# Reordering one core's instruction lists in an mLSTM and squared-ReLU kernel: scores ahead of attends, the tenth chunk's loads ahead of the eighth's x, joins ahead of squares, and another order of the PSUM banks

## The chip, the cores and the metric

The kernel runs on one core of a Trainium2 chip. A core has a matrix engine (TensorE, PE in the tables, with its weight loads listed apart as PEld), three engines that work on elements (VectorE or DVE, ScalarE or ACT, GpSimd or POOL), and SyncE (SP), which here issues all DMA transfers of the main part from one queue, in program order. Every engine carries out its own list of instructions strictly in order, and waits by semaphores for the others.

The metric is device microseconds of one launch. A chunk below is 128 rows of one batch's sequence with all 8 heads, a group is 256 tokens (two chunks) of the feed-forward part.

## The reference

Two stages run one after the other, all in float32.

```python
# mLSTM cell: B=4, H=8, S=768, D=40; for each t of the sequence, with a running stabiliser m
C = f_stab * C + i_stab * outer(v_t, k_t)
n = f_stab * n + i_stab * k_t
y_t = sigmoid(o_gate_t) * (C @ q_t) / max(|n . q_t|, 1)
# bridge: y (B, H, S, D) -> x (3072 tokens, 320)
# FFN: w_in (320, 2048), w_out (2048, 320)
out = relu(x @ w_in) ** 2 @ w_out
```

## The kernel before

**Chunks.** The recurrence over 768 steps is carried out in 6 chunks of 128 rows per batch, 24 in all, in order. For a chunk s the kernel loads k, q, v, the output gate and a row of decay sums A that is spread over all partitions (`load_A`, L334, tile A_bc, two buffers). POOL masks A (L359), and ACT makes W = exp(A + b) from it in 8 instructions (`weigh`, L383) and eA = exp(A) (`decays`, L369). PE multiplies k and q (`scores`, L423, into tile tp), DVE multiplies this by W (`weighted`, L436, two tiles P_sb), and PE multiplies P_sb by v and eA*q by the state C of the chunk before (`attend`; in the later form `attend_turned`, L522 with C, L511 for the new state, L533 with P_sb, into tile numT). The state moves on by C*decay plus the new products (L550, with POOL's `decay_C`, L489).

**The turned path.** From chunk 6 or 7 on, transposes are made with DMA and DVE. `pair_up` (4 DMAs, L287) copies k and q to a DRAM scratch, `load_squares` (4 DMAs, L309) brings them back in squares into kqT, one of two buffers, and `turn_kq` (DVE, L316) turns these. The attend's numerator goes numT, turned by DVE into tn (L544), `store_num` (L556) to DRAM, `load_num` (4 DMAs, L561) back, `normalise_turned` (DVE, L573 to L582) divides and applies the gate to give x_sb, `store_rows` (L608) and `load_rows` (4 DMAs, L613) bring x back as squares of xT, and `turn_squares` (DVE, L620) ends the turn. Then xT is ready for the feed-forward part.

**The feed-forward part.** FFN1 of a group has four steps (L644 with 32 and L655 with 16 matmuls in a batch, h_ps); ACT takes the relu into r_sb (L670), DVE the square into g (L677). FFN2 of group 0 is plain (L684). FFN2 of the other groups (`ffn2_fast`) makes the 2 by 2 block product with 7 products of 16 matmuls (L738), in four steps. These need sums of g (`sums`, L733) and of the weights (`sums_of_weights`, L712 to L719). The products go to two PSUM banks X and Y that are held through two steps; ACT copies (L758, L763) and DVE adds (L754) collect them in y_sb, which has three buffers for the two that a group uses. Steps 2 and 3 each store half of the group's result (L774, L779).

**Weights.** w_in and w_out are rounded while they come in, in 26 pieces. For a piece ACT makes two words (`words`, L195 and L197), DVE three steps and POOL the last add (`join`, L206, L210, L211, L215), and the fetch of a later piece follows on SP (L186).

**The order.** No scheduler moves anything: within each engine the order is that of the Python text. After a prologue, a loop `for u in range(8)` (L873) handles chunks 2 to 5, two turns for each, with FFN1 of groups 0 and 1 and the rounding of weights between. In it the three PSUM pools ps_at (3 banks), ps_h (3) and ps_o (2) are open. They are closed then, and ps_at and ps_h with 4 banks each follow. The second loop (L982) runs over a list of parts: n counts them, `which` is 1 for an FFN1 step and 2 for an FFN2 step. From n = 8 on, eight parts make a group's round: r = 0 and 1 are steps 0 and 1 of `ffn2_fast`, r = 2 to 5 the four FFN1 steps of the group two further, r = 6 and 7 the steps 2 and 3. FFN1 runs in pairs of steps: the matmuls L644 of both, L655 of both, and between them and the relus a "tiled" section, in which the attend of a chunk and the score of the next are placed. b = 7 + 2*(n//8) is the chunk of the round's first tiled section, b + 1 that of its second. The call `attended(s)` issues store_num, the next load of v and k, load_num and pair_up on SP. SP's and DVE's instructions in a round are thus in the order of the calls at r = 0 to 7.

Of the kernel before, what the change touches and what calls it, by code (L numbers as in the profile page):

```python
# [15 lines left out]
PSUM = bass.MemoryType.PSUM  # L16
# [13 lines left out]
def kernel(  # L30
# [49 lines left out]
    work = ctx.enter_context(tc.tile_pool(name="work", bufs=2))  # L80
    xts = ctx.enter_context(tc.tile_pool(name="xts", bufs=2))
    banks = ExitStack()
    ps_at = banks.enter_context(tc.tile_pool(name="ps_at", bufs=3, space=PSUM))
    ps_h = banks.enter_context(tc.tile_pool(name="ps_h", bufs=3, space=PSUM))
    ps_o = banks.enter_context(tc.tile_pool(name="ps_o", bufs=2, space=PSUM))
    ctx.enter_context(tc.manual_schedule())
    first = ExitStack()
    gates = first.enter_context(tc.tile_pool(name="gates", bufs=1))
# [225 lines left out]
    def turn_kq(s):  # L314
        t = kqT_b[s % NKT][:].rearrange("p n j t -> p (n j t)")
        nc.vector.transpose(t, t)  # L316
# [264 lines left out]
        nc.vector.tensor_tensor(x3, x3, dm[:].unsqueeze(2).to_broadcast([P, H, D]), op=ALU.mult)  # L581
        nc.vector.tensor_copy(x[:, DM:], x[:, DM - KR : DM])  # L582

    def normalise(s):
        d = st[s]
        num = d["num"]
        if num is not d["hp"]:
            nc.vector.tensor_tensor(num[:], num[:], d["hp"][:], op=ALU.add)
        dm = work.tile([P, H], F32, name="dm")
        nc.vector.tensor_scalar(dm[:], num[:, :, D], scalar1=-1.0, scalar2=1.0, op0=ALU.mult, op1=ALU.max)  # L590
        nc.vector.tensor_tensor(dm[:], dm[:], num[:, :, D], op=ALU.max)
        nc.vector.reciprocal(dm[:], dm[:])

        x = d["x"] = work.tile([P, 3 * P], F32, name="x_sb")
        x3 = x[:, :DM].rearrange("p (h d) -> p h d", d=D)
        nc.vector.tensor_tensor(x3, num[:, :, :D], d["og"], op=ALU.mult)
        nc.vector.tensor_tensor(x3, x3, dm[:].unsqueeze(2).to_broadcast([P, H, D]), op=ALU.mult)
        nc.vector.tensor_copy(x[:, DM:], x[:, DM - KR : DM])
# [183 lines left out]
    def do(f, s):  # L782
        if 0 <= s < NT:
            f(s)
# [66 lines left out]
    sigmoid(1)  # L851
    attend(0)
    rounding.step()
    normalise(0)
    mask(2)
    attend(1)
    normalise(1)
    load(3)
    load_A(3)
# [13 lines left out]
    for u in range(8):  # L873
        s = 2 + u // 2
        relu_half()
        if u % 2 == 0:
            if u == 0:
                ffn1(0, 0)
                scores(s)
                weighted(s)  # L880
                relu_half()
                rounding.step()
            else:
                turn_rows(s - 1)
                scores(s)
                ffn1(u // 4, u % 4)
            if u == 2:
                rounding.words()
            if u > 0:
                weighted(s)  # L890
            if u == 2:
                mask(s + 1)
                rounding.join()
                rounding.join()
                weigh(s + 1, masked=True)
                rounding.words()
            else:
                weigh(s + 1)
                if u > 0:
                    square_half()  # L900
        else:
            load_A(s + 2)
            for r in {1: (4,), 3: (5, 6), 5: (7,), 7: ()}[u]:
                load(r)
            if u == 5:
                for r in range(4, 8):
                    sigmoid(r)
            attend(s)
            if u in (1, 3):
                if u == 3:  # L910
                    square_half()
                normalise(s)
                rounding.join()
            else:
                rounding.join()
                normalise(s)
            for r in {5: (8,), 7: (9,)}.get(u, ()):
                load(r)
            for r in {5: (7,), 7: (8,)}.get(u, ()):
                pair_up(r)  # L920
            if u > 4:
                load_o(2 * s)
                load_o(2 * s + 1)
            transposes(s + 1)
            rounding.words()
            if u == 7:
                ffn1_main(1, 3)
                turn_rows(5)
                ffn1_rest(1, 3, st["half"][0])
            else:  # L930
                ffn1(u // 4, u % 4)
            square_half()
        if u < 4:
            load_o(4 + u)
        while rounding.done < NEXT[u]:
            rounding.step()
    relu_half()
    square_half()
    load_A(8)
    load_squares(7)  # L940
# [18 lines left out]
    assert LAST[-1] == len(pieces)  # L959


    def attended(s):
        do(store_num, s)
        do(load, s + 4)
        do(load_num, s)
        do(pair_up, s + 3)

    def ffn1_batch(g, i, tiled=lambda: None):
# [13 lines left out]
    for n, (which, g, i) in enumerate(parts):  # L982
# [11 lines left out]
        if n in (2, 5):  # L994
            attend_turned(s)
            decays(s + 1)
            mask(s + 1)
            if n > 4:
                turn_kq(s + 1)
            decay_C(s + 1)  # L1000
            if s > X_SQ:
                turn_squares(s - 1)
            attended(s)
        if n == 6:
            scale_q(s + 1)
        if 5 <= n < 8:
# [1 line left out]
        if n == 6:  # L1008
            sums(1, ALL, (1, 2))
        if n == 8:  # L1010
            decays(9)
            mask(9)
            turn_kq(9)
            load_squares(10)
            load_A(10)
            sums_of_weights(3)
            sums(1, ALL, (3,))
        if n == 9:
            attend_turned(8)
            score(9)  # L1020
            decay_C(9)
            attended(8)
            turn_squares(7)
# [3 lines left out]
        if r == 0 and g > 1:  # L1027
            do(turn_squares, b - 2)
            sums(g, ALL, (3,))
        elif r == 1 and g > 1:  # L1030
            do(turn_squares, b - 1)
        elif r == 4:
            do(scale_q, b + 1)
            do(turn_kq, b + 2)
        elif r == 5:
            do(normalise_turned, b)
            do(store_rows, b)
        elif r == 7 and g < NG - 1:
            sums(g + 1, ALL, (2,))
            do(normalise_turned, b + 1)  # L1040
            do(store_rows, b + 1)
# [5 lines left out]
        if which == 1:  # L1047
            ffn1_main(g, i)
            if i % 2 == 0:
                st["held"] = st["half"]  # L1050
            elif r is None:
                ffn1_batch(g, i)
                if n != 3:
                    square_half()
                    square_half()
            else:
                x = b + i // 2

                def tiled():
                    do(attend_turned, x)  # L1060
                    do(score, x + 1)

                ffn1_batch(g, i, tiled)
                do(decay_C, x + 1)
        elif g == 0:
            ffn2(g, *divmod(i, 2))
        else:
            ffn2_fast(g, i)

        if n in (2, 6):  # L1070
            masked_W(s + 1)
            if n < 4:
                turn_kq(s + 1)
                scale_q(s + 1)
            normalise_turned(s)
            store_rows(s)
            load_squares(s + 2)
            load_rows(s)
            load_A(s + 2)
        if n == 7:  # L1080
            for t in range(8, 12):
                sigmoid(t)
        if n == 8:
            masked_W(9)
        elif n == 9:
            load_A(11)
            load_o(12)
            load_o(13)
            decays(10)
            mask(10)  # L1090
        elif n == 10:
            normalise_turned(8)
            store_rows(8)
        if r == 0 and g > 1:
            do(decays, b + 1)
            do(mask, b + 1)
            square_half()
        elif r == 1:
            if g > 1:
                do(pair_up, b + 2)  # L1100
            square_half()
            if g < NG:
                sums(g, ALL, (4,))
            do(scale_q, b)
            do(turn_kq, b + 1)
        elif r == 2:
            do(masked_W, b + 1)
            do(load_squares, b + 2)
            if n == 10:
                load_rows(8)  # L1110
        elif r == 3:
            do(decays, b + 2)
            do(mask, b + 2)
            attended(b)
            if b % 4 == 3:
                for t in range(b + 1, min(b + 5, NT)):
                    sigmoid(t)
        elif r == 4:
            square_half()
            square_half()  # L1120
            do(masked_W, b + 2)
            do(load_A, b + 3)
        elif r == 5:
            do(store_num, b + 1)
            do(load_rows, b)
            do(load_num, b + 1)
            do(load, b + 5)
            for t in range(b + 5, min(b + 7, NT)):
                load_o(t)
        elif r == 6:  # L1130
            do(load_squares, b + 3)
        elif r == 7:
            do(load_A, b + 4)
            do(load_rows, b + 1)
# [35 lines left out]
```

## Time and profile before

| | us |
|---|---|
| median of 8 runs | 537.05 |
| lowest, highest run | 533.98, 537.86 |
| the profiled run, whole time | 537.25 |
| span of its records | 535.5 |
| PE busy (share of the span) | 515.9 (96%) |
| PEld busy | 449.0 (84%) |
| DVE busy | 329.2 (61%) |
| ACT busy | 192.4 (36%) |
| POOL busy | 88.1 (16%) |
| mean granted clock of PE | 0.984 |

The profile is of one execution. The span is the time from its first to its last record; the run's time holds 1.75 us more. A row of a timeline gives the start, the length, the engine, the line of the kernel, the operation with the tile that it writes and the tiles that it reads, the number of instructions joined in the row (x16), and in brackets the idle time of the engine ahead of them and what ended it. PEclk is the clock that PE was granted, 1.00 being full speed. The chain of waits is followed backwards from the end: each piece is what the next one waited for.

### The profile page before, as it was taken

To read this page: it belongs to the slowest core of one execution; us is meant where nothing else is said; L and a number is where in the kernel's file an instruction comes from. 1 tells how busy PE (TensorE), PEld (TensorE's weight loads), DVE (VectorE), ACT (ScalarE), POOL (GpSimd) and SP (SyncE) were. 2 spreads that over 40 slices of the span, in tenths; PEclk is the share of its full clock that TensorE was granted. 3 is DMA by queue.
4 is the path that set the end of the run, shared out by engine and by line. 5 is a ranking of instruction groups with operands and counts; after the bars stand their busy time and mean duration, and the time that the engine had idled before them with its cause. 6 is when DMAs were issued, how large, how long until landed. Compare 5 with 4: busy or idle time off the path is not lost.

```text
span 535.5 us, 10368 instructions
## 1 busy us (share of the span) xinstructions
PE 515.9 (96%) x3932; PEld 449.0 (84%) x3933; DVE 329.2 (61%) x638; ACT 192.4 (36%) x460; POOL 88.1 (16%) x110
## 2 busy tenths in 40 slices
PE   9997999999949999999999999999999999999997
PEld 4875888786748898897897898897898898998997
DVE  8579988769744773664764773764764764341451
ACT  3776486361534403713413703413613301102100
POOL 3346653221202110110110110100200100000000
PEclk9998899999969999999999999999999999999999
DMA  9999698967487775776775785775673230200000
GB/s 197 219 197 203 153 192 187 206 149 148 100 165 164 160 143 118 157 133 128 156 136 121 156 141 120 167 130 126 155 155 63 76 87 21 63 12 1 26 26 24
DMA packets 239394, 68.06 MB, mean 127 GB/s; under 512 B 185744, under 2 KB 233872, under 8 KB 239344
## 3 DMA queue, kind: packets, MB, share of 16 engines
q1 hardware_dynamic: 239248, 67.20, 60.0%
q8 instruction: 31, 0.51, 0.4%
q10 hardware_dynamic: 96, 0.20, 0.1%
q14 instruction: 19, 0.16, 0.1%
HBM read 55.08 MB, written 17.86 MB: 136 GB/s over the span
## 4 chain that ended last, share of the span: by engine, by line
PE 67%; DMA 15%; DVE 7%; SPq 6%; issue 3%; ACT 1%; POOL 0%; DVEq 0%; POOLq 0%; ACTq 0%
PE h_ps L644 23%; PE h_ps L738 22%; PE h_ps L655 7%; DMA x_rows<-x_sb 4%; PE tp L423 3%; SPq L613 3%; DMA xT<-x_rows 3%; DMA out_dram<-y_sb 2%; DMA kq<-num_rows 2%; PE numT L533 2%; PE hp L459 2%; DMA A_bc<-a_rows 2%; PE idle L797 2%; PE numT L522 1%; DMA num_rows<-tn 1%
## 5 line engine op out<-in xcount | busy, mean ns | idle before, releaser
L644 PE MATMUL h_ps<-xT,w_in 128*128 128x256 f32 x768 | 175.8, 385 | 7.3 <-POOL w_in L215 3.4
L644 PEld LDWEIGHTS h_ps<-xT,w_in 128*128 128x128 f32 x768 | 144.9, 192 | 30.8 <-DVE y_sb L754 5.2
L670 ACT ACTIVATE r_sb<-h_ps 128x512 f32<-128x512 f32 x96 | 49.8, 598 | 126.7 <-PE h_ps L655 74.2
L738 PE MATMUL h_ps<-w_out,g 128*128 128x160 f32 x528 | 77.7, 305 | 3.4 <-ACT y_sb L758 3.4
L738 PEld LDWEIGHTS h_ps<-w_out,g 128*128 128x128 f32 x528 | 75.0, 195 | 3.8 <-ACT y_sb L758 3.7
L677 DVE TENSOR_TENSOR g<-r_sb 128x512 f32<-128x512 f32 x96 | 64.4, 721 | 11.7 <-ACT r_sb L670 11.6
L383 ACT ACTIVATE W_sb<-A_bc,b_T 128x128 f32<-128x128 f32 x176 | 53.8, 388 | 21.2 <-POOL A_bc L359 21.0
L738 PE MATMUL h_ps<-T,S 128*128 128x160 f32 x352 | 52.3, 302 | 0.0
L738 PEld LDWEIGHTS h_ps<-T,S 128*128 128x128 f32 x352 | 48.8, 190 | 1.5 <-ACT r_sb L670 0.7
L655 PE MATMUL h_ps<-xT,w_in 64*128 64x256 f32 x384 | 49.0, 391 | 0.0
L655 PEld LDWEIGHTS h_ps<-xT,w_in 64*128 64x128 f32 x384 | 34.8, 186 | 12.1 <-issue 9.1
L754 DVE TENSOR_TENSOR y_sb<-y_sb,h_ps 128x160 f32<-128x160 f32 x44 | 13.8, 315 | 45.9 <-PE h_ps L738 45.9
L359 POOL TENSOR_SCALAR_AFFINE_SELECT A_bc<-A_bc 128x1024 f32<-128x1024 f32 x22 | 25.5, 1160 | 83.4 <-ACT kq L369 72.9
L758 ACT COPY y_sb<-h_ps 128x160 f32<-128x160 f32 x11 | 3.2, 293 | 99.8 <-PE h_ps L738 99.8
L544 DVE STREAM_TRANSPOSE tn<-numT 128x256 f32<-128x256 f32 x36 | 15.6, 446 | 37.8 <-PE numT L533 37.2
L436 DVE TENSOR_TENSOR P_sb<-tp,W_sb 128x512 f32<-128x512 f32 x46 | 29.7, 686 | 10.2 <-PE tp L423 6.8
L620 DVE STREAM_TRANSPOSE xT<-xT 128x384 f32<-128x384 f32 x18 | 10.3, 572 | 41.3 <-DMA xT<-x_rows 41.3
L423 PE MATMUL tp<-kqT 40*128 40x128 f32 x384 | 28.7, 290 | 4.6 <-issue 3.4
L423 PEld LDWEIGHTS tp<-kqT 40*128 40x128 f32 x384 | 24.4, 193 | 8.9 <-issue 6.4
L395 POOL TENSOR_TENSOR vw<-va,W_sb 128x328 f32<-128x328 f32 x20 | 16.8, 839 | 84.1 <-ACT W_sb L383 73.1
L738 PE MATMUL h_ps<-w_out,S 128*128 128x160 f32 x176 | 25.7, 299 | 0.0
L738 PE MATMUL h_ps<-T,g 128*128 128x160 f32 x176 | 25.7, 299 | 0.0
(119 smaller groups left out, 592.3 us busy)
## 6 DMA issues: line engine op xcount, KB each, us to landing
A_bc<-a_rows SPq DMA_DIRECT2D x23, 512.0 KB, 5.2
raw<-in_moe_w_out_dram SPq DMA_DIRECT2D x16, 320.0 KB, 3.5
num_rows<-tn SPq DMA_DIRECT2D x18, 256.0 KB, 2.3
kq<-num_rows SPq DMA_DIRECT2D x72, 64.0 KB, 2.1
kqT<-kq_rows SPq DMA_DIRECT2D x34, 128.0 KB, 3.2
raw<-in_moe_w_in_dram SPq DMA_DIRECT2D x8, 512.0 KB, 4.9
kq<-in_k_dram SPq DMA_DIRECT2D x24, 160.0 KB, 3.8
va<-in_v_dram SPq DMA_DIRECT2D x24, 160.0 KB, 4.1
```

The lines of the kernel that those rows point to most:

```text
L359: nc.gpsimd.affine_select(A[:], A[:], compare_op=ALU.is_ge, fill=-1e30, base=0, pattern=[[0, H], [1, P]], channel_multiplier=-1,)
L383: nc.scalar.activation(d["W"][:, i * n + h, :], A[i][:, h, :], AF.Exp, bias=b_T[:, b, c, i * n + h : i * n + h + 1],)
L395: nc.gpsimd.tensor_tensor(d["vw"][:], d["va"][:], d["W"][:, :, P - 1 : P].to_broadcast([P, H, D1]), op=ALU.mult,)
L423: nc.tensor.matmul(sc[i][:, j, :], lhsT=d["kT"][rows, j, :], rhs=d["qT"][rows, j, :], start=True, stop=True,)
L436: nc.vector.tensor_tensor(t, d["sc"][i], d["W"][:, heads, :], op=ALU.mult)
L544: nc.vector.transpose(to[:, 2 * i : 2 * i + 2], numT[i][:, :2, :].rearrange("p c t -> p (c t)"))
L613: nc.sync.dma_start(t[r * SQ : (r + 1) * SQ].rearrange("p (b a) -> p b a", a=SQ), x_d[s, :, :, r * SQ : (r + 1) * SQ].rearrange("c (n p) a ...
L644: nc.tensor.matmul(hs[i][:, n, :], lhsT=w_in[:, a, fb * P : (fb + 1) * P], rhs=xT[:, :, a, :], start=(n == 0 and a == 0), stop=False,)
L655: nc.tensor.matmul(hs[i][:, n, :], lhsT=w_in2[rows, 2 * pp + n, :], rhs=xT[rows, :, 2, :], start=False, stop=(n == 1),)
L670: nc.scalar.activation(rs[-1][:], h[:], AF.Relu)
L677: nc.vector.tensor_tensor(g4[:, :, i, :], r[:], r[:], op=ALU.mult)
L738: nc.tensor.matmul(to, lhsT=lhsT[:, p], rhs=rhs[:, p, :], start=(start and p == 0), stop=(p == NPAIR - 1), skip_group_check=True,)
```

## The change

The change adds and removes no instruction. It moves them within the engines' lists, and opens the PSUM pools in another order.

- PSUM pools of the first loop: ps_o is opened first, then ps_at, ps_h. The banks are then o 0-1, at 2-4, h 5-7 instead of at 0-2, h 3-5, o 6-7. The second loop's pools lie at banks 0-3 and 4-7 in both, so another bank follows each of the old ones.
- First loop: `sum_of_h` is split off `normalise`, and stands ahead of the join where the join now stands ahead of the rest of normalise (u = 1 as well as 5 and 7). At u = 1 the squares follow the joins of the weights. At u = 7 the last square and relu come ahead of the words.
- The tenth chunk (s = 9): its `load_squares` and `load_A` are issued by `attended(7, early=True)`, after load_num(7) and ahead of pair_up(10), of a store of y, and of store_rows(7) and load_rows(7). Its `decays`, `mask` and `turn_kq` are called at the end of part 7 instead of in part 8.
- `score` stands ahead of `attend_turned` in part 9 and in each tiled section, so the scores' matmuls and DVE's two P_sb are ahead of the attend's matmuls, its two tn and the update of C.
- `turn_squares(b - 1)` moves from part r = 1 to r = 2, after masked_W and load_squares.

```diff
+    ps_o = banks.enter_context(tc.tile_pool(name="ps_o", bufs=2, space=PSUM))
     ps_at = banks.enter_context(tc.tile_pool(name="ps_at", bufs=3, space=PSUM))
     ps_h = banks.enter_context(tc.tile_pool(name="ps_h", bufs=3, space=PSUM))
-    ps_o = banks.enter_context(tc.tile_pool(name="ps_o", bufs=2, space=PSUM))
...
-            if u in (1, 3):
-                if u == 3:
-                    square_half()
+            if u == 3:
+                square_half()
+            sum_of_h(s)
+            if u == 3:
                 normalise(s)
-                rounding.join()
-            else:
-                rounding.join()
+            rounding.join()
+            if u != 3:
                 normalise(s)
...
                 ffn1_rest(1, 3, st["half"][0])
+                square_half()
+                relu_half()
             else:
                 ffn1(u // 4, u % 4)
-            square_half()
+                if u > 1:
+                    square_half()
...
         while rounding.done < NEXT[u]:
             rounding.step()
-    relu_half()
+        if u == 1:
+            square_half()
     square_half()
...
-    def attended(s):
+    def attended(s, early=False):
         do(store_num, s)
         do(load, s + 4)
         do(load_num, s)
+        if early:
+            load_squares(s + 2)
+            load_A(s + 2)
         do(pair_up, s + 3)
...
-            attended(s)
+            attended(s, early=(n == 5))
...
         if n == 8:
-            decays(9)
-            mask(9)
-            turn_kq(9)
             load_squares(10)
...
         if n == 9:
+            score(9)
             attend_turned(8)
-            score(9)
...
-        elif r == 1 and g > 1:
-            do(turn_squares, b - 1)
...
                 def tiled():
+                    do(score, x + 1)
                     do(attend_turned, x)
-                    do(score, x + 1)
...
             store_rows(s)
-            load_squares(s + 2)
+            if n == 2:
+                load_squares(s + 2)
             load_rows(s)
-            load_A(s + 2)
+            if n == 2:
+                load_A(s + 2)
         if n == 7:
             for t in range(8, 12):
                 sigmoid(t)
+            decays(9)
+            mask(9)
+            turn_kq(9)
...
             do(load_squares, b + 2)
+            if g > 3:
+                do(turn_squares, b - 1)
```

More of the change, by code (lines that the diff above doesn't have):

```diff
@@ L582, in normalise_turned, with sum_of_h @@
         nc.vector.tensor_copy(x[:, DM:], x[:, DM - KR : DM])
-    def normalise(s):
+    def sum_of_h(s):
         d = st[s]
@@ L588, in normalise @@
             nc.vector.tensor_tensor(num[:], num[:], d["hp"][:], op=ALU.add)
+    def normalise(s):
+        d = st[s]
+        num = d["num"]
         dm = work.tile([P, H], F32, name="dm")
@@ L853 @@
     rounding.step()
+    sum_of_h(0)
     normalise(0)
@@ L856 @@
     attend(1)
+    sum_of_h(1)
     normalise(1)
```

## Prediction

> **What bounds the kernel now.** I read the page first. TensorE (PE) is busy almost throughout, so other engines count only where PE waits for them.
>
> ```profile
> PE 515.9 (96%) x3932; PEld 449.0 (84%) x3933; DVE 329.2 (61%) x638; ACT 192.4 (36%) x460; POOL 88.1 (16%) x110
> PE   9997999999949999999999999999999999999997
> PEclk9998899999969999999999999999999999999999
> ```
>
> A slice is 13.4 us. Slices 4 and 12 (PE 7 and 4) stand out, and the granted clock sinks around both. So next I read PE's timeline for its idle times, and for records slower than their own pace (L644 0.216 us each, L738 16 in 2.17, L423 16 in 1.09).
>
> ```profile
> 50.18 1.22 PE L644 MATMUL h_ps<-xT,w_in 128*128 128x256 f32 x2 [2.20 <-POOL w_in L215]
> 52.65 5.11 PE L644 MATMUL h_ps<-xT,w_in 128*128 128x256 f32 x14 [1.25 <-POOL w_in L215]
> ...
> 99.50 1.16 PE L423 MATMUL tp<-kqT 40*128 40x128 f32 x16 [1.25 <-ACT r_sb L670]
> ...
> 152.16 2.17 PE L423 MATMUL tp<-kqT 40*128 40x128 f32 x16 [3.35 <-issue]
> 157.70 6.79 PE L738 MATMUL h_ps<-w_out,g 128*128 128x160 f32 x32 [3.36 <-ACT y_sb L758]
> 164.33 7.07 PE L644 MATMUL h_ps<-xT,w_in 128*128 128x256 f32 x32
> ...
> 249.04 1.99 PE L644 MATMUL h_ps<-xT,w_in 128*128 128x256 f32 x8 [0.93 <-DVE y_sb L754]
> ```
>
> There are four kinds of loss: weights at 50, a bank at 98, the tenth chunk at 149 to 164, and a short wait in the first FFN1 part of a steady group. 14 L644 in 5.11 instead of 14 x 0.216 = 3.02 is the halved clock. The busy times by stretch (length, PE, PEld, DVE, ACT, POOL, PEclk, DMA share, GB/s) show what precedes it:
>
> ```profile
> 46.10:49.50 3.40, 1.88 (x23) 1.28 (x19) 3.37 (x4) 2.30 (x5) 3.32 (x4) 1.00 1.26 170
> 49.50:56.40 6.90, 4.97 (x11) 3.54 (x12) 6.76 (x9) 3.83 (x8) 4.45 (x4) 0.51 0.59 168
> 97.30:100.70 3.40, 2.15 (x25) 1.58 (x25) 2.07 (x5) 3.40 (x9) 1.24 (x3) 1.00 0.65 123
> ```
>
> A stretch of 3.4 us with PE busy 1.88 (idle 1.52) was followed by half speed, one with 2.15 (idle 1.25) was not. A fall cost 2.1 at 50 (5.11 - 3.02) and 3.4 at 152 (L423 2.17 - 1.09, L738 6.79 - 4.34).
>
> [...]
>
> **A. Joins ahead of squares (25 to 56 us).** FFN1(0,2) waits for w_in pieces 5 and 6: 2.2 and 2.0 idle, 2.1 by the clock. Joins 6 and 7 now precede the two L677 (45.61 to 47.99). But POOL's add of piece 5 stands behind vw, Cd and C (L395, L473, L478, 45.15 to 48.73) whatever DVE does, and ACT's words for piece 6 end at 46.6. [...] Ends: 0.3 (POOL's queue alone rules) and 4 (idle also falls under 1.5 and the clock stays: 1.9 + 2.1). L206 took 1.10 and L210 1.37 beside POOL, against 0.42 and 0.43 for the same forms alone; the joins stay in that company, so I stay near the low end. Squares 2.4 later are covered: their first reader (FFN2) is 50 us on.
>
> [...]
>
> **B. Bank order and relu first.** score(6) at 99.50 waits 1.25 for the relu whose bank it takes; that relu stood behind two `words` on ACT. Now it takes another bank, freed by ACT's copy of xT at 97.7, and follows L655 at 98.18: gain 1.3 (0.5 if the next FFN1 meets the second relu at 99.2). Elsewhere banks rotate with the same depth: 0.
>
> **C. The tenth chunk.** The chain of waits names it:
>
> ```profile
> 143.72 0.38 SPq L608
> ...
> 147.36 0.61 SPq L613
> ...
> 150.42 4.27 DMA A_bc<-a_rows
> ...
> 156.05 0.64 ACT kq L369
> 156.70 0.63 ACT kq L369
> 157.35 0.30 ACT y_sb L758
> 157.70 6.79 PE h_ps L738 x32
> ```
>
> SP is stuck at store_rows(7) (L608) until x is ready at 143.72, and squares(9) (4 L309) and A(9) (L334) stand behind it. So turn_kq(9) waits until 150.82 and score(9) to 152.16; exp(A) begins at 156.05, and on ACT the y_sb copy, which step 1's product needs, stands behind it. PE loses 3.35 + 1.08 + 3.36 + 2.3 = 10.1. After, the five issues (3.10 + 0.47) follow load_num(7) at 136.5: L309 to 139.6, L334 to 140.1, landing (4.3 to 5.4) 144.4 to 145.5. turn_kq(9) (1.25) follows L716 at 145.1 to 146.4, before score(9) at 146.8. ACT ends the sigmoids at 144.6, then table load and L369 (2.6) to 148, the copy to 148.3; attend(8) follows score(9), to 149.9; step 1 runs 149.9 to 154.2. POOL's mask (1.1) and W(9) (2.44) end at 151.5, P_sb(9) at 152.5. xT(7) is the next due: pair_up(10) and L692 (3 us) now fill SP's idle time 139.7 to 143.7, L608 is hardly later, L613 loses the 3.1 of L309 ahead of it but waits for x_rows, and the turn ends near 154. FFN1(3,0) starts at 154.2 to 154.7 instead of 164.33: gain 9.8 (5 if these loads land at 149, where score(9) waits 2 and the clock falls).
>
> Then SP must carry the same transfers in 10 us less. It is almost full from 130 to 190, so y stores and the next loads fall behind in the first group: I give back 2.0 (0 to 4.5; the upper end is SP's own idle time of 4.06 at 139.66 to 143.72, used up).
>
> **D. turn_squares(b-1) from step 1 to after masked_W.** L620 stood ahead of the y_sb add and waited for xT's landing:
>
> ```profile
> 208.60 0.58 DVE L620 STREAM_TRANSPOSE xT<-xT 128x384 f32<-128x384 f32 x1 [7.51 <-DMA xT<-x_rows]
> 209.10 0.28 DVE L754 TENSOR_TENSOR y_sb<-y_sb,h_ps 128x160 f32<-128x160 f32 x1
> ...
> 240.09 0.33 DVE L754 TENSOR_TENSOR y_sb<-h_ps,y_sb 128x160 f32<-128x160 f32 x1 [1.05 <-DMA out_dram<-y_sb]
> ```
>
> The first FFN1 part lacks the bank that this add frees. From x24 at 203.65 to x8 at 209.44 is 5.79, 24 x 0.216 = 5.18: 0.61 lost; in the next groups 1.09, 1.12, 0.40, 0.89. Gain 4.1. Its reader is the next group, so its new place, behind turn_kq(b+1) (213.5), costs nothing.
>
> **E. Score ahead of attend.** PE's work is the same. On DVE the two P_sb(b+1) come ahead of tn(b), and take over the two buffers that attend(b)'s L533 reads. In the group at 213.29 (end of the first L655): score to 214.38, attend to 215.6, then P_sb 1.29, then tn 0.89: end 218.1 instead of 215.48, so 2.65 later. On this path hang, by the chain of waits: num_rows 3.21, L561 on SP, kq 2.43, normalise 2.3, x_rows 3.75, L613 on SP, L561, and behind them on SP the y1 store (L774) at 236.76, landing 3.20. The third row above waits for that landing, as y_sb has three buffers, and step 1's second product needs the add: it ended at 240.42 for a product at 240.60, and in the next groups 0.6, 1.9, 0.9, 1.9, 1.9 ahead. With 1.9 to 2.65 more: 0.9 to 2.3 of PE wait at this group, 0.2 to 1.8, 0 to 1.5, 0.6 to 1.6, then none (no o_gate loads ahead of the store). Ends 1.7 and 7.2, taken 4.4. A wait past 1.5 may also halve the clock (2.1 to 3.4).
>
> **Sum.** -1.0 - 1.3 - 9.8 - 4.1 + 2.0 + 4.4 = -9.8. The profiled execution took 537.25 (span 535.5 and 1.75 around it), 0.2 over the median of 537.05: 537.25 - 9.8 = 527.5 us.
>
> **Rivals.**
> - *E costs nothing* (0.25). SP has idle stretches before L613, and the store may be issued as early as now. Then 537.25 - 16.2 + 2.0 = 523; with A's clock kept (-3) 520. Against it: slack of 0.2 in the group at 240.
> - *SP decides* (0.15). C's loads land at 149 (gain 5), the backlog gives back 4.5, E 4.4, others as forecast: -1.0 - 1.3 - 5 - 4.1 + 4.5 + 4.4 = -2.5: 534.7; with half of C's shortfall 532.
> - *Slower* (0.07). Step 1's wait for the y1 store is worst in all four groups (7.2), and each wait takes a half-clock window with it (4 x 2.8), with the backlog at 4.5: 22.9 against 16.2 gained, 544. It decides from the third fall of the clock on (4.5 + 7.2 + 3 x 2.8 = 20.1, over 16.2 + 1.6). For it: 1.52 idle was enough at 49. Against it: only the first group reaches 1.5 by my middle values.
> - *It does not do what it says* (0.04). The early loads wait for a buffer of kqT or A_bc still read, so C remains, with D paid out by E: about 537. Against it: the last readers of both buffers, W(7) and score(7), end at 119.4 and 121.
>
> **How the numbers follow.** Forecast 527.5 with 0.49. The likeliest cases reach from 520 to 532; with the SP case's 534.7 the range is 519 to 535.5, leaving out the slower and the nothing case and A's and E's best ends together. About 0.3% (1.6 us) is what a measurement of this kernel can tell from no change: faster 0.89 (the first three), same 0.04 (the last), slower 0.07.
>
> **What would show it.** PE's L423 after 146.8 without idle, and no half clock at 152: C. L754 of step 0 directly behind its product and no idle ahead of the x8 of L644: D. A wait of L738 for DVE L754, in turn for out_dram<-y_sb, near 230, 270 and 310: E. The two waits for L215 hardly shorter: A. It is wrong if the loads of chunk 9 land after 147, or if clocks fall in the steady groups.

## The result, and the profile after

| | before | after |
|---|---|---|
| median, us | 535.93 (32 runs) | 529.48 (11 runs) |
| lowest, highest | 533.98, 538.2 | 526.14, 533.69 |
| profiled execution, us | 537.25 | 526.66 |
| span, mean granted clock | 535.5, 0.984 | 524.9, 0.993 |
| PE, DVE, POOL busy | 515.9, 329.2, 88.1 | 510.4, 334.0, 92.2 |

The ratio of the medians is 0.9879 with a 95% interval of 0.9858 to 0.9900: the change takes 6.5 us off. The two profiled executions differ by more, 10.6 us, because the one after is among the quick ones. The executions after spread over 7.5 us, and their granted clock goes with it: 0.996 at 526.1 and 526.3, 0.990 to 0.994 at 528 to 531.5, 0.984 at 533.7. In the clock records of the two profiles the half speed is 0.50; by that, as an estimate, a mean of 0.984 instead of 0.996 is 0.012 x 525 / 0.5 = 12.6 us more at half speed, where up to half is lost. The ratios below leave out one execution of the run y_early (533.8), which lies over 1.5% above the fastest of its kernel.

Lines below L588 have moved by 4 (L644 is L648, L738 is L742, L754 is L758). PE's timeline of the kernel after, the rows that answer to those of before:

```profile
49.20 0.98 PE L648 MATMUL h_ps<-xT,w_in 128*128 128x256 f32 x2 [1.25 <-POOL w_in L215]
51.66 5.56 PE L648 MATMUL h_ps<-xT,w_in 128*128 128x256 f32 x14 [1.48 <-POOL w_in L215]
...
98.95 7.17 PE L648 MATMUL h_ps<-xT,w_in 128*128 128x256 f32 x32 [0.33 <-ACT r_sb L674]
...
145.14 1.16 PE L423 MATMUL tp<-kqT 40*128 40x128 f32 x16
...
148.16 4.61 PE L742 MATMUL h_ps<-w_out,g 128*128 128x160 f32 x32
152.86 7.17 PE L648 MATMUL h_ps<-xT,w_in 128*128 128x256 f32 x32
...
174.42 1.26 PE L423 MATMUL tp<-kqT 40*128 40x128 f32 x16 [0.60 <-PE h_ps L659]
...
193.90 2.44 PE L742 MATMUL h_ps<-w_out,g 128*128 128x160 f32 x16 [3.05 <-DVE y_sb L758]
...
232.54 2.44 PE L742 MATMUL h_ps<-w_out,g 128*128 128x160 f32 x16 [0.36 <-DVE y_sb L758]
...
271.98 2.44 PE L742 MATMUL h_ps<-w_out,g 128*128 128x160 f32 x16 [0.25 <-DVE y_sb L758]
...
311.38 2.44 PE L742 MATMUL h_ps<-w_out,g 128*128 128x160 f32 x16 [0.21 <-DVE y_sb L758]
...
351.56 2.44 PE L742 MATMUL h_ps<-w_out,g 128*128 128x160 f32 x16 [1.90 <-DVE y_sb L758]
```

The two long idle times and the half clock around 152 to 164 (0.50 from 151.9 to 162.2 before, 1.00 from 152 to 157 after) are gone, and so are the waits of the L648 x8. New are the waits of step 1's second product (L742) for DVE's add: the mechanism that part E forecast, and ahead of them one of 3.05 at 193.90, for which E had no term (C's "I give back" had one).

The matmuls of the feed-forward part have the same order in both kernels, so the start of the same matmul in both traces gives a ledger. FFN1(g,p) is the first layer of group g from its step p on, "gained" how much sooner a place is reached, "step" what was gained since the row above:

| place | before | after | gained so far | step |
|---|---|---|---|---|
| end of FFN1(0,2) (A) | 57.68 | 57.16 | 0.5 | 0.5 |
| FFN1(2,0) (B) | 100.60 | 98.95 | 1.6 | 1.1 |
| FFN1(3,0) (C) | 164.33 | 152.86 | 11.5 | 9.8 |
| second product, first group | 201.47 | 193.90 | 7.6 | -3.9 |
| the same, next groups | 240.60 | 232.54 | 8.1 | 0.5 |
| | 281.11 | 271.98 | 9.1 | 1.1 |
| | 321.65 | 311.38 | 10.3 | 1.1 |
| | 360.46 | 351.56 | 8.9 | -1.4 |
| end | 532.33 | 521.75 | 10.6 | 1.7 |

Within a group the same comparison, read every 16 matmuls, separates D from E: 0.72, 1.19, 1.22, 0.40 and 0.99 gained where the L644 x8 had waited (D), 0.52, 0.41, 0.38 and 2.06 lost at the second product (E), and 0.20 gained at each of 13 tiled sections, which nothing in the prediction had.

### The profile page after: what moved, and what is told of

The parts are those of the page before. It is cut to its first block, busy times and chain, and to the rows that moved or that the text cites. A ratio compares the mean times of both kernels' runs of the same rounds, so it can differ in the third digit from the quotient of the medians.

```text
span 524.9 us, 10358 instructions
## 1 busy us (share of the span) xinstructions
PE 510.4 (97%) x3932; PEld 448.0 (85%) x3933; DVE 334.0 (64%) x638; ACT 194.0 (37%) x460; POOL 92.2 (18%) x110
## 4 chain that ended last, share of the span: by engine, by line
PE 69%; DMA 12%; SPq 8%; DVE 6%; issue 2%; ACT 2%; POOL 1%; DVEq 0%; ACTq 0%; POOLq 0%
PE h_ps L648 25%; PE h_ps L742 19%; PE h_ps L659 7%; DMA out_dram<-y_sb 3%; DMA kq<-num_rows 3%; PE tp L423 3%; SPq L561 3%; PE h_ps L688 3%; DMA num_rows<-tn 3%; DMA x_rows<-x_sb 2%; SPq L617 2%; PE hp L459 2%; PE numT L533 2%; PE idle L801 2%; PE numT L522 1%
## 5 line engine op out<-in xcount | busy, mean ns | idle before, releaser
L648 PE MATMUL h_ps<-xT,w_in 128*128 128x256 f32 x768 | 174.8, 385 | 3.8 <-POOL w_in L215 2.7
L648 PEld LDWEIGHTS h_ps<-xT,w_in 128*128 128x128 f32 x768 | 145.4, 192 | 26.4 <-POOL w_in L215 3.6
L742 PE MATMUL h_ps<-w_out,g 128*128 128x160 f32 x528 | 76.9, 300 | 5.8 <-DVE y_sb L758 5.8
L742 PEld LDWEIGHTS h_ps<-w_out,g 128*128 128x128 f32 x528 | 73.0, 190 | 7.3 <-DVE y_sb L758 7.0
L681 DVE TENSOR_TENSOR g<-r_sb 128x512 f32<-128x512 f32 x96 | 68.7, 766 | 10.0 <-ACT r_sb L674 10.0
L742 PE MATMUL h_ps<-T,S 128*128 128x160 f32 x352 | 52.3, 302 | 0.0
L742 PEld LDWEIGHTS h_ps<-T,S 128*128 128x128 f32 x352 | 48.8, 190 | 1.6 <-ACT r_sb L674 0.8
L659 PE MATMUL h_ps<-xT,w_in 64*128 64x256 f32 x384 | 49.0, 391 | 0.0
L659 PEld LDWEIGHTS h_ps<-xT,w_in 64*128 64x128 f32 x384 | 34.8, 186 | 12.1 <-issue 9.1
L758 DVE TENSOR_TENSOR y_sb<-y_sb,h_ps 128x160 f32<-128x160 f32 x44 | 14.1, 320 | 47.0 <-PE h_ps L742 47.0
L359 POOL TENSOR_SCALAR_AFFINE_SELECT A_bc<-A_bc 128x1024 f32<-128x1024 f32 x22 | 29.4, 1334 | 68.9 <-ACT kq L369 67.5
L395 POOL TENSOR_TENSOR vw<-va,W_sb 128x328 f32<-128x328 f32 x20 | 17.7, 887 | 77.2 <-ACT W_sb L383 62.9
L489 POOL TENSOR_TENSOR Cd<-C,kq 128x164 f32<-128x164 f32 x15 | 7.0, 464 | 118.6 <-DVE C L550 104.9
L423 PEld LDWEIGHTS tp<-kqT 40*128 40x128 f32 x384 | 24.8, 188 | 3.3 <-issue 1.1
L423 PE MATMUL tp<-kqT 40*128 40x128 f32 x384 | 26.4, 276 | 0.6 <-PE h_ps L659 0.6
L369 ACT ACTIVATE kq<-A_bc 64x512 f32<-64x512 f32 x30 | 18.8, 628 | 19.7 <-DMA A_bc<-a_rows 17.8
L742 PE MATMUL h_ps<-T,g 128*128 128x160 f32 x176 | 25.7, 299 | 0.0
L742 PE MATMUL h_ps<-w_out,S 128*128 128x160 f32 x176 | 25.7, 299 | 0.0
```

What stands on the lines that cost most here:

```text
L359: nc.gpsimd.affine_select(A[:], A[:], compare_op=ALU.is_ge, fill=-1e30, base=0, pattern=[[0, H], [1, P]], channel_multiplier=-1,)
L369: nc.scalar.activation(e[rows], st[s]["A"][0][rows, PR * i : PR * (i + 1), :], AF.Exp)
L395: nc.gpsimd.tensor_tensor(d["vw"][:], d["va"][:], d["W"][:, :, P - 1 : P].to_broadcast([P, H, D1]), op=ALU.mult,)
L423: nc.tensor.matmul(sc[i][:, j, :], lhsT=d["kT"][rows, j, :], rhs=d["qT"][rows, j, :], start=True, stop=True,)
L648: nc.tensor.matmul(hs[i][:, n, :], lhsT=w_in[:, a, fb * P : (fb + 1) * P], rhs=xT[:, :, a, :], start=(n == 0 and a == 0), stop=False,)
L659: nc.tensor.matmul(hs[i][:, n, :], lhsT=w_in2[rows, 2 * pp + n, :], rhs=xT[rows, :, 2, :], start=False, stop=(n == 1),)
```

## The experiments

Ratios are to the kernel before on the same chip, with 95% intervals. "The first group" is that of FFN1(3,0) and the FFN2 steps behind it. What it "gives back" is the time from the start of FFN1(3,0) to step 1's second product, less the 37.14 (201.47 - 164.33) of before; it is 3.90 (193.90 - 152.86 - 37.14) in the profile above.

**after_again**, the changed kernel once more.

> The changed kernel itself, for another profile of it and as the base for the runs beside it. Both theories: about 529.5 us. In its profile the five waits of PE for DVE's y_sb add (3.05, 0.36, 0.25, 0.21, 1.90 us in the first profile) come again, each within 1.5 us of its first value; if this execution is slower than 526.7, the granted clock is lower in proportion (0.01 of mean clock, 5 us at half speed more, is worth 2 to 2.6 us).

0.9869 (0.9825 to 0.9913); the profiled execution took 531.02. Four waits came again (2.45, 1.06, 0.22, 1.92), the fifth was under 0.2. The first group gave back 6.6, as the score at 175.95 waited 2.40 instead of 0.60 and the clock fell behind it (0.76 from 175 to 182; the 16 of L533 at 178.30 took 1.96 instead of 1.07). PE's timeline of this execution has a row that the first profile has at full speed:

```profile
354.25 3.75 PE L742 MATMUL h_ps<-w_out,g 128*128 128x160 f32 x16 [1.92 <-DVE y_sb L758]
```

16 in 3.75 instead of 2.44: here the clock fell behind the wait of 1.92 (0.93 from 350 to 356, 0.74 from 356 to 361). In the first profile, with 1.90, it stayed at 1.00 (351 to 356). Such falls, there in one execution and absent in another, are a likely source of the spread; the executions without a profile can't show it.

**attend_first**, E undone (here in the tiled sections; part 9 likewise).

```diff
-                    do(score, x + 1)
                     do(attend_turned, x)
+                    do(score, x + 1)
```

> The changed kernel with part E undone: attend ahead of score again in part 9 and in each tiled section. Theory 1 (E makes tn, and through SP's list the y1 store, 2 to 2.6 us late): the five waits shrink from 5.8 in sum to 1.5 or less, while the 0.2 us that each tiled section had gained comes back as a loss (13 x 0.2 = 2.6); 526.5 to 528.5. Rival (SP's list is overfull after the tenth chunk's gain, E has no part in it): the 3.05 stays above 2.5, and the time is 530 to 532.

0.9845 (0.9802 to 0.9888), no different from the changed kernel within the intervals. Against the first profile the ledger shows +0.20 at each tiled section, and -0.52, -0.42, -0.38, -2.06 at the second products: so much of theory 1 holds. But the first group gave back 9.0:

```profile
176.43 0.67 PE L522 MATMUL numT<-kq,C 40*64 40x128 f32 x16 [2.60 <-DVE kq L484]
...
185.61 2.44 PE L742 MATMUL h_ps<-w_out,S 128*128 128x160 f32 x16 [1.54 <-DVE y_sb L758]
...
198.79 3.82 PE L742 MATMUL h_ps<-w_out,g 128*128 128x160 f32 x16 [4.22 <-DVE y_sb L758]
```

So the 3.05 in the first group is not E's: without E it is 4.22. There the rival was right, and the median of 530.71 lies in its 530 to 532.

**y_early**, the y1 store sooner on SP.

```diff
             do(load_num, b + 1)
-            do(load, b + 5)
-            for t in range(b + 5, min(b + 7, NT)):
-                load_o(t)
         elif r == 6:
+            do(load, b + 5)
+            for t in range(b + 5, min(b + 7, NT)):
+                load_o(t)
```

> The changed kernel with the loads of v, k and the output gates of part r = 5 issued after step 2 of the FFN2 and not before it, so that SP issues the y1 store (L778) right behind load_num(b+1), 2.0 to 4 us sooner in the four groups that load gates. Theory 1 (the store's place in SP's list makes PE wait): waits of 3.05 and 1.90 fall below 1, the three of 0.2 to 0.4 vanish; 524 to 526. Rival (the landing itself, or another reader of the bank, holds the add): waits change by less than 0.5, 529 to 530.

0.9784 (0.9735 to 0.9833), which is lower than after_again's, but the two intervals overlap. In the profiled execution the three larger waits remained, 3.64, 0.61 and 2.12. The store was issued right behind load_num as meant (345.33), so its place alone does not make PE wait.

**four_y**, four y_sb tiles from a pool that has room, used in turn.

```diff
-            st["y"] = [ffn.tile([P, DM], F32, name="y_sb", bufs=3) for _ in range(2)]
+            st["y"] = [next_y() for _ in range(2)]
```

> The changed kernel with four y_sb buffers instead of three, so that step 0's add (u12) writes a buffer whose store landed a group before. Theory 1: the five waits for DVE's y_sb add vanish (5.8 us in the profiled execution), and with them what they cost in clock in other executions; 523 to 525. Rival (the add is late for another reason: DVE's place behind normalise and sums): at least half of the waits remain, 527 to 530.

0.9759 (0.9720 to 0.9799): the median is 5.6 us under after_again's on the same chip, and the intervals do not meet, so the fourth buffer is worth something in this kernel. Its profiled execution (529.95) is the slowest of six. In it the waits at 194, 272 and 311 are gone; 0.52 at 235 and 2.13 at 353 are not, and in the first group the score waits 2.78 at 177.11 instead. DVE's timeline tells why the wait at 353 stays:

```profile
348.30 1.11 DVE L573 TENSOR_SCALAR dm<-kq 128x8 f32<-128x8 f32 x1 [4.48 <-DMA kq<-num_rows]
...
352.78 0.32 DVE L767 TENSOR_TENSOR y_sb<-h_ps,y_sb 128x160 f32<-128x160 f32 x1
```

normalise(b+1) (L573 and on) stands ahead of the add (here L767) on DVE, and waits for the landing of num(b+1), the same late chain. The add has two predecessors that E delays, the store and this one; I had seen one. With the store out of the way the other still holds it at 353.

**tn_first**, PE in the new order, DVE in the old (part 9 likewise).

```diff
-                    do(score, x + 1)
+                    do(scores, x + 1)
                     do(attend_turned, x)
+                    do(weighted, x + 1)
```

> The changed kernel with the scores' matmuls still ahead of the attend's on PE, but on DVE tn(b) and the update of C ahead of the two P_sb(b+1). Theory 1 (E's cost is DVE's order, its small gain is PE's order): the 0.2 us of each tiled section stays, and of the waits for DVE's y_sb add those in the groups at 232, 272, 311 and 351 vanish, as with attend first; the first group's stays at 2 to 4.5. About 3 us under the changed kernel of the same chip (ratio to before 0.980 to 0.983). Rival (the gain of 0.2 came with DVE's order, or a tn 1.1 us later than before is still too late): either the sections take 0.2 us longer again, or 0.2 to 1 us of wait remains in at least three of these groups.

0.9776 (0.9737 to 0.9814). The 0.20 of each section stays, the waits at 232, 272 and 311 vanish, and of that at 351 remains 1.62, where a gate load ahead of the y1 store took 2.07 us to issue on SP. So the small gain belongs to PE's order and the three small losses to DVE's; the largest, at 351, stays with DVE in the old order, and whose it is this run leaves open. The first group gave back 7.5.

**c_only**, C alone on the kernel before.

> The kernel before with part C alone. Theory 1: PE's loss from 148.65 to 164.33 goes (9.9 us by step 1's start of FFN1), and 4 to 5.5 come back in the first group, from SP's list: a wait of the score near 174 and of step 1's second product near 195, without E. Ratio to before 0.988 to 0.992. Rival (the first group's waits are E's work): the first group gives back less than 2, and the ratio is 0.981 to 0.985.

0.9957 (0.9930 to 0.9985): C alone is worth 2.3 us. Its ledger shows 10.0 gained at step 1's two products ahead of FFN1(3,0), and 8.0 given back in the first group, with 1.65 more just behind it, where 16 of L738 took 4.03 (the third row):

```profile
179.20 0.67 PE L522 MATMUL numT<-kq,C 40*64 40x128 f32 x16 [1.54 <-DVE kq L484]
...
188.14 2.44 PE L738 MATMUL h_ps<-w_out,S 128*128 128x160 f32 x16 [1.31 <-DVE y_sb L754]
...
201.70 4.03 PE L738 MATMUL h_ps<-w_out,g 128*128 128x160 f32 x16 [4.61 <-DVE y_sb L754]
```

The mechanism was as expected; its size, 8.0 and 1.65, was about twice the 4 to 5.5 that I took.

**sp_light**, two gate loads moved from part 9 to part 12.

> The changed kernel with the gate loads of chunks 12 and 13 (two L324, 2.36 us of SP) issued in part 12 instead of part 9, behind the squares of chunk 11 and the x of chunk 8. Theory 1 (in the first group SP's list is the bound): x store, squares(11) and num(9) are issued 2 to 2.4 us sooner, the score's wait near 174 falls to 0 from 0.6 to 2.8, the y_sb wait near 194 falls below 1.5; 3 to 4 us under the changed kernel. Rival (the landing times of the transfers, shared among 16 engines, are the bound, and not their issue): waits change by less than 1 us.

0.9894 (0.9860 to 0.9928). The score waited 0.70 (0.60 and 2.40 in the two profiles of the changed kernel), and the add's wait rose to 5.03 (from 3.05 and 2.45). On SP the moved loads (179.55 to 181.7) now stood ahead of the store of x of chunk 9, ready at 179.8 and issued at 181.83. The work was moved from one place of the same late chain to another. This run could not decide between the theories.

**fill**, matmuls on zeros ahead of the waits at 48 to 53.

```diff
+        if (g, pp) == (0, 2):
+            fill(4)
...
+                if (g, pp) == (0, 2) and (i, n) == (0, 1):
+                    fill(6)
```

> The changed kernel with 4 and 6 matmuls on zeros (128x512, into a bank of ps_o) ahead of the two waits of FFN1(0,2) for the weights' adds, so that PE is busy in most of the 1.25 and 1.48 us. It computes nothing that is used. Theory 1 (a wait of 1.2 to 1.8 us here halves the clock): the 14 matmuls after the second wait take 3.0 to 3.3 us instead of 4.7 to 5.6, and no half clock shows between 48 and 60; 1.5 to 2.5 us under the changed kernel. Rival (the clock falls here for another reason than idle time): 14 in 4.7 to 5.6 as before, time as the changed kernel's.

0.9867 (0.9794 to 0.9941), nothing gained. My second fill was misplaced: the wait of 1.77 lies between the two matmuls ahead of it, so it remained, and the six fills ran behind it at half speed (2.68 for six). The clock fell for one stretch (51.6 to 55.0 at 0.53) after one with PE busy 1.52 of 3.4. It settles nothing about what a well placed fill is worth.

**e_only**, E alone on the kernel before.

> The kernel before with part E alone. Theory 1: waits of step 1's second product for DVE's y_sb add appear in the groups at 240, 281 and 321 (0.2 to 1 each) and at 360 (1 to 2.3), sum 2.5 to 4.5, against 2.6 gained from PE's order in 13 sections: within 2 us of before, ratio 0.997 to 1.004. Rival (E is the source of the change's gain): ratio under 0.993.

1.0183 (1.0142 to 1.0224): 10 us slower, far outside what either theory gave. DVE's and PE's timelines show where it goes:

```profile
212.50 0.58 DVE L620 STREAM_TRANSPOSE xT<-xT 128x384 f32<-128x384 f32 x1 [7.34 <-DMA xT<-x_rows]
213.01 0.28 DVE L754 TENSOR_TENSOR y_sb<-y_sb,h_ps 128x160 f32<-128x160 f32 x1
...
216.14 1.24 DVE L316 STREAM_TRANSPOSE kqT<-kqT 128x1024 f32<-128x1024 f32 x1
```

```profile
204.02 3.82 PE L738 MATMUL h_ps<-w_out,g 128*128 128x160 f32 x16 [3.08 <-DVE y_sb L754]
...
213.34 1.99 PE L644 MATMUL h_ps<-xT,w_in 128*128 128x256 f32 x8 [0.33 <-DVE y_sb L754]
...
217.48 1.26 PE L423 MATMUL tp<-kqT 40*128 40x128 f32 x16 [0.22 <-PE h_ps L655]
...
337.26 1.99 PE L644 MATMUL h_ps<-xT,w_in 128*128 128x256 f32 x8 [1.90 <-DVE y_sb L754]
...
370.68 2.44 PE L738 MATMUL h_ps<-w_out,g 128*128 128x160 f32 x16 [1.92 <-DVE y_sb L754]
```

With turn_squares (L620) still in step 1, DVE stands still for the landing of x ahead of the add and of turn_kq (L316), and the score, which is now first in its section, follows that turn (L316 ends at 217.38, the score starts at 217.48). So two things that I had left out take part: the five sections behind the x8 take 0.38 longer each where with D they took 0.20 less, and the waits that D removes grow by 1.6 in sum (1.8 at 337, and 0.2 less in the four others together). But of the 9.5 in this ledger the larger part is lost at second products, 4.7 in the first group (3.08 of wait, then 16 in 3.82) and 2.1 at 370. There the kernel with all five parts waits as well (3.05 and 1.90), so E's own cost is not explained by D's absence alone.

**best**, tn_first, four_y and y_early together, and turn_squares(8) behind turn_kq(11) in part 12.

> The changed kernel with four edits of the runs before together: DVE's tn ahead of P_sb, four y_sb buffers, the loads of part r = 5 behind the y1 store, and turn_squares(8) in part 12 behind scale_q and turn_kq instead of ahead of them. Theory 2 (the first group gives back because x of chunk 8 lands late, and DVE's list puts turn_squares(8) ahead of scale_q(10) and turn_kq(11); the y_sb add waits for the y1 store and for normalise(b+1)): the score's wait near 175 falls below 0.5, the y_sb add's waits to at most 1.7 in one or two groups; 5 to 8 us under the changed kernel, ratio to before 0.970 to 0.976. Rival (the DMA landings themselves set the pace in the first group, so the wait only moves to the next step): 2 to 4 us remain in the first group, ratio 0.976 to 0.980.

0.9770 (0.9727 to 0.9814). The score's wait at 175 is gone, no group after the first waits, and the first group gave back 6.4: it waits for y_sb adds instead.

```profile
183.04 2.44 PE L751 MATMUL h_ps<-w_out,S 128*128 128x160 f32 x16 [2.43 <-DVE y_sb L767]
...
195.95 4.63 PE L751 MATMUL h_ps<-w_out,g 128*128 128x160 f32 x16 [3.94 <-DVE y_sb L767]
```

The rival held in that the wait moved to the next step, and in the ratio; it had put 2 to 4 us in the first group.

**c_freed**, the same freeing on top of C alone.

> The kernel before with part C, four y_sb buffers and turn_squares(8) behind turn_kq(11). Theory 2: of the 9.5 us that the first group gave back with C alone, 6 to 8 stay gained; ratio to before 0.980 to 0.985. Rival (landings set the pace): the first group gives back 5 or more all the same; ratio 0.988 to 0.994.

0.9956 (0.9932 to 0.9979), as C alone. The first group gave back 6.3 up to the second product. The waits moved:

```profile
188.41 4.12 PE L747 MATMUL h_ps<-w_out,S 128*128 128x160 f32 x16 [3.37 <-DVE y_sb L763]
...
199.85 2.44 PE L747 MATMUL h_ps<-w_out,g 128*128 128x160 f32 x16 [0.80 <-DVE y_sb L763]
...
211.08 1.99 PE L644 MATMUL h_ps<-xT,w_in 128*128 128x256 f32 x8 [3.61 <-DVE y_sb L763]
```

Their sum is 7.8 where c_only had 7.5 (1.54, 1.31, 4.61). The third stands behind turn_squares (L620), which this kernel, without D, has in step 1, and which waited 9.25 for the landing of x. Theory 2 falls: neither turn_squares(8) in DVE's list nor the lack of a fourth y_sb buffer was the cause.

**pair_act**, tn_first and four_y, and pair_up issued by ACT.

```diff
-                nc.sync.dma_start(
+                (nc.scalar if s > 9 else nc.sync).dma_start(
                     kq_d[s, i, n]...
```

> The changed kernel with DVE's tn ahead of P_sb, four y_sb buffers, and the copies of k and q to the scratch (pair_up, four DMAs of 0.6 us of SP for a chunk, from chunk 10 on) issued by ACT instead of SP. Theory 3 (in the first group SP's list is the bound: 54 issues and 32.7 us of issuing in 43.3 us, where a later group has 46 in 39): 5 us of SP's 32.7 go, x of chunk 8 and num(9) are issued 2 to 4 us sooner, and the first group gives back 2 to 4 instead of 4 to 7.6; ratio to before 0.970 to 0.975. Rival (the landings, 2 to 5 us each in a chain of five, set the pace): the first group gives back 4.5 or more; ratio 0.976 to 0.980.

0.9665 (0.9625 to 0.9705), 18 us under the kernel before, and the lowest ratio of all. PE's timeline after 126 has two idle times left:

```profile
145.86 1.25 PE L423 MATMUL tp<-kqT 40*128 40x128 f32 x16 [0.22 <-PE h_ps L751]
...
175.45 1.25 PE L423 MATMUL tp<-kqT 40*128 40x128 f32 x16 [1.09 <-issue]
```

The first group gave back 1.1. The gain is larger than theory 3 gave. From FFN1(3,0) to the end of step 1's second product SP has 45 issues with 26.3 us of issuing; the eleven other profiles of kernels with C have 53 to 57 there with 32 to 36 us, and the kernel before, which has no such waits, 48 with 28.1. It is the only run in which the first group's loss does not reappear. That speaks for theory 3. It also puts these copies into a second queue (q10 moved 4.79 MB, and 0.20 in the changed kernel), and the runs do not tell the shorter list from the second queue.

## Why the prediction was right, and where it was not

527.5 was forecast from a profiled execution of 537.25; the profiled one after took 526.66, the median is 529.48, and the range held it. By the medians the change is worth 6.5 of the 9.8 forecast; the profiled executions differ by 10.6. That the sum came so near is in part luck: 2.6 us from PE's order, for which there was no term, made up for 1.9 more given back in the first group and 0.7 less from A and B.

- **A**, forecast 1.0, got 0.5. The 1.0 has pieces 5 and 6 at 49.6 and 51.6 (from 50.13 and 52.59), my estimates, for which no run shows the ground; in the profile the matmuls that need them start at 49.20 and 51.66, against 50.18 and 52.65 before. But the stretch at half speed stayed where it was, 49.53 to 56.36 before and 49.47 to 56.30 after by the traces' clock records. The 14 matmuls began 1.0 sooner, ran 0.9 longer in it and took 5.56 instead of 5.11, so half of the lead was lost. Nor does the clock stay when the idle time falls under 1.5 in such a stretch, as A's upper end had it: after, PE was busy 2.16 of the 3.41 us up to 49.47, and the clock fell; before, it was busy 2.16 of the 3.41 up to 100.72, and it did not fall. Piece 5's lead was twice the 0.5 that I gave it: POOL's queue is not fixed, and its work ran faster, as its timelines before and after show:

```profile
45.15 1.15 POOL L395 TENSOR_TENSOR vw<-va,W_sb 128x328 f32<-128x328 f32 x1 [2.56 <-ACT W_sb L383]
46.26 1.18 POOL L473 TENSOR_TENSOR Cd<-C_sb,dec 128x328 f32<-128x328 f32 x1
47.52 1.21 POOL L478 TENSOR_TENSOR C_sb<-C_sb,Cd 128x328 f32<-128x328 f32 x1
```

```profile
45.34 0.74 POOL L395 TENSOR_TENSOR vw<-va,W_sb 128x328 f32<-128x328 f32 x1 [2.56 <-ACT W_sb L383]
46.04 0.74 POOL L473 TENSOR_TENSOR Cd<-C_sb,dec 128x328 f32<-128x328 f32 x1
46.85 0.88 POOL L478 TENSOR_TENSOR C_sb<-C_sb,Cd 128x328 f32<-128x328 f32 x1
```

  Before, DVE squared (L677) from 45.61 to 47.99 beside these; after, it was idle from 45.4 to 47.0, and POOL's L395 took 0.74 instead of 1.15, its L473 0.74 instead of 1.18. No run moved the squares alone, so that they were the cause was not shown. I had weighed the joins that came next to POOL (L206 1.10, L210 1.37) and not the squares that went.
- **B**, 1.3 forecast, 1.1 measured; 0.33 for the second relu remained, the lower bound's reason.
- **C**, 9.8 forecast and 9.8 measured, and score(9), attend(8) and step 1 followed each other without idle time, as described. What failed is the term after it, "I give back 2.0 (0 to 4.5)": 3.9 in the profiled execution, 3.4 to 7.5 in the other runs with C, score first and pair_up on SP, and 8.0, 9.0 and 6.3 in those with attend first (c_only, attend_first, c_freed). c_only shows whose it is: with C alone 8.0 of 10.0 came back, so the cover for late loads in this group had been PE's idle time itself. I had priced SP's lag by SP's idle time of 4.06. c_freed and best show that a wait taken away here came back elsewhere, and pair_act that most of it goes with four copies per chunk off SP; whether by the shorter list or by the second queue stays open.
- **D**, 4.1 forecast, 4.5 measured, without a new wait. D was not run by itself. E cost 10 us alone and nothing that shows beside A to D; which of them makes the difference was not tried.
- **E**, 4.4 forecast. 3.4 was lost at four second products (0.52, 0.41, 0.38, 2.06, forecast 0.9 to 2.3, 0.2 to 1.8, 0 to 1.5, 0.6 to 1.6, so the first and the last lie outside), and 13 x 0.2 = 2.6 was gained, from PE's order, for which I had said "PE's work is the same". The mechanism (tn later, and all behind it) was right, the store as its only carrier was wrong: four_y, without the wait for the store, still has 2.13 behind normalise. In the first group, where E had no term, attend first gave back more in two of three runs; why that is was not tried by itself. Undone, E changes nothing that the intervals can show.
- **Clock.** The clock risk that I gave E's waits was real: the median lies 2.8 above the profiled execution, in which no clock fell between the stretch at 50 and the last products. By the prediction's own sign ("wrong ... if clocks fall in the steady groups") it was wrong in other executions: from 350 to 400 the granted clock was 0.97 in after_again, y_early and four_y, with waits of 1.92, 2.12 and 2.13 there, and 1.00 in the first profile, with 1.90. (The prediction puts the fall at 152 at 3.4 us; its two differences, 1.08 and 2.45, make 3.5.)
- The rival "slower" had the right place and price. By its own count it needed three falls of the clock besides the worst waits; the profiled executions with E show none to two beyond that at 50.

## What to carry to other kernels

A big idle time can be somebody's cover (with C alone 8.0 of 10.0 us came back): ask what SP and the DMA queues did in it, and price the group after it, not only the stall itself. Where several waits hung on one chain of DMAs, taking away one at a time moved the wait to the next (7.5 us of waits in c_only, 7.8 in c_freed); giving independent copies to an engine with time to spare (ACT, busy 37%), which shortened SP's issuing in the first group to 26.3 us from 32 and opened a second queue, was here the edit after which it did not come back (1.1 given back). A move can cost much alone and nothing beside others (E alone cost 10 us, with A to D it was neutral), so price a move in the order of instructions that it will run in.

## What was not expected of the hardware

- The order of the small matmuls cost time by itself here. The section from L655 to the next L644 took 4.64 before (211.36 to 216.00), and 4.45 after, with the same matmuls:

```profile
203.17 2.00 PE L659 MATMUL h_ps<-xT,w_in 64*128 64x256 f32 x16
205.00 1.06 PE L423 MATMUL tp<-kqT 40*128 40x128 f32 x16
205.99 0.67 PE L522 MATMUL numT<-kq,C 40*64 40x128 f32 x16
206.59 1.09 PE L533 MATMUL numT<-P_sb,va 128*64 128x128 f32 x16
```

  The 16 of L423 take 1.06 behind L659 and took 1.16 behind L533, and L659 hands over 0.1 sooner than to L522. The contraction rows are 64, 40, 40, 128 here, and 64, 40, 128, 40 before: one change fewer. But the sections without L522 (the one from 214.72 to 218.87 after) gained the same 0.20, and there the count is the same, 64, 40, 128, 128 and 64, 128, 128, 40. So the reason stays open.
- Waits of like length were followed by a slower clock in one execution and not in another. Near 354 one of 1.92 was followed by 16 products in 3.75 (after_again), one of 1.90 by 16 in 2.44 (after). In the first group 16 of them took 3.82 behind 3.08 (e_only) and 2.44 behind 3.64 (y_early). So the length of the wait alone does not tell. The clock records before and after show three stretches at half speed (0.50) between 10 us and the last products: 6.83 at 49.53 and 10.24 at 151.93 before, 6.83 at 49.47 after.
- Half of the DMA issues on SP between 150 and 360 us take up to 0.51 us and nine in ten up to 0.84 (after), but nine of 250 took 1.3 to 2.0 (a gate load 1.89 at 188.82), on an engine that spent 32 of 43 us issuing in the first group; one of y_early took 2.16 (the x store at 163.99).
